# Head of a fused linear-attention and MLP kernel: values before the folded key weights

## The chip, the cores and the metric

The kernel runs on 1 core of a Trainium2 chip. The core has TensorE (PE), VectorE (DVE), ScalarE (ACT), GpSimd (POOL) and SyncE (SP), which run their own instruction queues and wait for one another by semaphores; DMAs are issued from SP's and ScalarE's queues here. The metric is the device time of one execution in microseconds, the median over runs. A measurement here tells differences of about 0.2% from none.

## The reference

Two branches read the same layer-normalised rows and are added to the input:

```python
def _A_ref(x, wqkv, w_phi, wo):
    B, S, D = x.shape
    H = 32; Dh = D // H
    qkv = (lambda x, *d: x.transpose(*d))((x @ wqkv).reshape(B, S, 3, H, Dh), 2, 0, 3, 1, 4)
    q, k, v = qkv[0], qkv[1], qkv[2]
    pq = jnp.einsum("bhsd,hdf->bhsf", q, w_phi)
    pk = jnp.einsum("bhsd,hdf->bhsf", k, w_phi)
    phi_q = jnp.concatenate([_softmax(pq, axis=-1), _softmax(-pq, axis=-1)], axis=-1)
    phi_k = jnp.concatenate([_softmax(pk, axis=-1), _softmax(-pk, axis=-1)], axis=-1)
    kv = jnp.einsum("bhsf,bhsd->bhfd", phi_k, v)
    z  = jnp.einsum("bhsf->bhf", phi_k)
    num = jnp.einsum("bhqf,bhfd->bhqd", phi_q, kv)
    den = jnp.einsum("bhqf,bhf->bhq", phi_q, z)[..., None] + 1e-6
    o = num / den
    return (lambda x, *d: x.transpose(*d))(o, 0, 2, 1, 3).reshape(B, S, D) @ wo

def _B_ref(x, w1, b1, w2):
    h = jnp.einsum("bsd,df->bsf", x, w1) + b1
    sp = jnp.log1p(jnp.exp(-jnp.abs(h))) + jnp.where(h > 0, h, jnp.zeros_like(h))
    act = h * jnp.tanh(sp)
    return jnp.einsum("bsf,fd->bsd", act, w2)

x = A_x
xn = _layernorm(x, axis=-1)
return x + _A_ref(xn, A_wqkv, A_w_phi, A_wo) + _B_ref(xn, B_w1, B_b1, B_w2)
```

S = 2048 rows, D = 512, 32 heads of 16, F = 1792, all bf16. The activation of the second branch is Mish.

## The kernel before

The 2048 rows are 16 tiles of 128, in 4 groups of 4. Everything stays on the core; only x and the weights come in and the result goes out. The order of the instructions on every engine is the order in which the code issues them (a manual schedule), so an instruction that waits holds back all that is issued behind it on its engine.

**The head (from line 420).** SP's queue issues x tiles 0 and 1, the key weights turned by a transposing DMA (`load_turned`), x tiles 4 to 7, the value weights `wv`, the first MLP weights `w1_sb`, and x tiles 8 to 15. ScalarE's queue issues `wsrc` (the per-head 16x16 maps), x tiles 2 and 3, and the bias `b1b`. GpSimd makes the identity and `block`, the mask of 16x16 blocks. VectorE copies three masks from `block`, and multiplies `block` with `wsrc` to the block-diagonal `Wbd`. TensorE runs 12 matmuls on the identity whose result nobody reads (`warm`). Then `fold` multiplies the turned key weights with `Wbd` to `wkp`, so that the key logits come out of one projection: 16 matmuls of 128 columns in four PSUM banks, each copied out.

`ln_stats` takes the layer norm's statistics on VectorE, and the power -1/2 on GpSimd; `ln_apply` applies them (on VectorE for groups 0 and 1, on GpSimd after). `ln_turn_pe` turns a tile by four TensorE transposes into a PSUM bank and a copy; from group 1 on, `normal` applies and turns by DMA. `project` is four matmuls of 512 columns: a tile's key logits (`logits`, with `wkp`) or its values (`value`, with `wv`, copied into `vext`). `hidden(n)` issues n units of the MLP's first layer: four matmuls of 512 columns and a Mish on ScalarE. There are 56 such units in all, and the calls share them out between the stages.

**The stages (loop from line 498).** For stage s, `exponentials(s)` takes the exponentials of a group's logits on ScalarE (two instructions for the halves k = 0, 1), `accumulate(s - 1)` adds a group's keys times values (32 matmuls of 129 columns), then come the values of group s (two tiles copied by VectorE, two by ScalarE), the logits of group s + 1, the statistics of group s + 2, `normalise` (a reduction, a reciprocal and a product on VectorE, for each half), the hidden units and `extremes(s + 1)`: the running max and min of the softmaxes, ten VectorE instructions in two planes. In stage 0 all four values of group 0 are done ahead of the loop, `extremes(0)` has `normal` of group 1 between its planes, and three tiles of the next logits go to a wide PSUM tile.

After the loop come the queries, the attention and the output projection, and the MLP's second layer; the change does not touch them.

**PSUM.** It has 8 banks. The pool `ps` has 5, handed out in turn to every projection, fold, transpose and hidden unit; the pool `ps2` has 3, for the wide tiles. An allocation waits until the bank's last content was copied out.

Of the kernel before, what the change touches and what calls it, by code (L numbers as in the profile page):

```python
# [8 lines left out]
BF16 = mybir.dt.bfloat16  # L9
FP32 = mybir.dt.float32  # L10

ACT = mybir.ActivationFunctionType
ALU = mybir.AluOpType
# [4 lines left out]
def kernel(  # L18
# [38 lines left out]
    vpool = ctx.enter_context(tc.tile_pool(name="vpool", bufs=1))  # L57
    opool = ctx.enter_context(tc.tile_pool(name="opool", bufs=2))
    ps = ctx.enter_context(tc.tile_pool(name="ps", bufs=5, space=bass.MemoryType.PSUM))
    ps2 = ctx.enter_context(tc.tile_pool(name="ps2", bufs=1, space=bass.MemoryType.PSUM))  # L60

    x_sb = persist.tile([P, NT, D], BF16, name="x_sb")
    xnT = persist.tile([P, NT, KT, P], BF16, name="xnT")
# [11 lines left out]
    wqp = wqk[:, :, 0:D]  # L75
    wo_sb = wqk[:, :, D : 2 * D]
    ident = consts.tile([P, P], BF16, name="ident")
    mhalf = consts.tile([P, TPG], FP32, name="mhalf")
    block = consts.tile([P, 8, 16], BF16, name="block")
    KVmask = consts.tile([P, 136], FP32, name="KVmask")  # L80
# [12 lines left out]
    def fold(wT, dst, dve):  # L93

        for kt in range(KT):
            pf = ps.tile([P, 512], FP32, name="pfold", tag="mm")
            for j in range(4):
                nc.tensor.matmul(
                    pf[:, j * P : (j + 1) * P],
                    lhsT=wT[:, j, kt * P : (kt + 1) * P],  # L100
                    rhs=Wbd[:, j, :],
                    start=True,
                    stop=True,
                )
            if kt in dve:
                nc.vector.tensor_copy(dst[:, kt, :], pf[:])
            else:
                nc.scalar.copy(dst[:, kt, :], pf[:])

    def ln_stats(t0, n):  # L110

        stats = lnp.tile([P, TPG, nc.vector.BN_STATS_DIM], FP32, name="stats")
        mv = lnp.tile([P, TPG, nc.vector.BN_AGGR_DIM], FP32, name="mv")
        rstd = lnp.tile([P, TPG], FP32, name="rstd")
        for i in range(n):
            nc.vector.bn_stats(stats[:, i, :], x_sb[:, t0 + i, :])  # L116
        for i in range(n):
            nc.vector.bn_aggr(mv[:, i, :], stats[:, i, :])
        nc.gpsimd.tensor_scalar(
            out=rstd[:, 0:n], in0=mv[:, 0:n, 1], scalar1=1e-5, scalar2=None, op0=ALU.add  # L120
        )
        nc.gpsimd.tensor_tensor(out=rstd[:, 0:n], in0=rstd[:, 0:n], in1=mhalf[:, 0:n], op=ALU.pow)
        return mv, rstd

    def ln_apply(t0, n, mv, rstd, xn, at):
        engine = nc.gpsimd if t0 > TPG else nc.vector
        for i in range(n):
            engine.tensor_scalar(  # L128
                out=xn[:, at + i, :],
                in0=x_sb[:, t0 + i, :],  # L130
                scalar1=mv[:, i, 0:1],
                scalar2=rstd[:, i : i + 1],
                op0=ALU.subtract,
                op1=ALU.mult,
            )

    def ln_turn_pe(t, xn, i, copy):
        ptr = ps.tile([P, 512], BF16, name="ptr", tag="mm")
        for kt in range(KT):
            nc.tensor.transpose(  # L140
                ptr[:, kt * P : (kt + 1) * P], xn[:, i, kt * P : (kt + 1) * P], ident[:]
            )
        copy(xnT[:, t, :, :], ptr[:].rearrange("p (k c) -> p k c", k=KT))
# [7 lines left out]
    def project(w, t, pp=None):  # L151

        if pp is None:
            pp = ps.tile([P, 512], FP32, name="pproj", tag="mm")[:]
        for kt in range(KT):
            nc.tensor.matmul(  # L156
                pp, lhsT=xnT[:, t, kt, :], rhs=w[:, kt, :],
                start=(kt == 0), stop=(kt == KT - 1),
            )
        return pp  # L160

    def value(t, copy):
        pv = project(wv, t)
        copy(
            vext[(t // TPG) % 2][:, t % TPG, :, 0:128], pv.rearrange("p (j c) -> p j c", j=4)
        )
# [3 lines left out]
    def hidden(n):  # L170

        for _ in range(n):
            g, f = next(units)
            ph = ps.tile([P, 512], FP32, name="ph", tag="mm")
            for kt in range(KT):
                nc.tensor.matmul(  # L176
                    ph[:],
                    lhsT=w1_sb[:, kt, f * P : (f + 1) * P],
                    rhs=xnT[:, g * TPG : (g + 1) * TPG, kt, :],
                    start=(kt == 0),  # L180
                    stop=(kt == KT - 1),
                )
            nc.scalar.activation(  # L183
                acts[:, f, g * 512 : (g + 1) * 512], ph[:], ACT.Mish, bias=b1f[:, f : f + 1]
            )
# [4 lines left out]
    def logits(s, i, copy):  # L190
        if i == 0:
            p_of[s] = smx.tile([P, TPG, 512], BF16, name="p_sb", bufs=1)
        pp = project(wkp if s < NG else wqp, (s % NG) * TPG + i)
        copy(p_of[s][:, i, :], pp)  # L194
# [222 lines left out]
        queue.dma_start(o_v[:, t, c], y)  # L417


    nc.sync.dma_start(x_sb[:, 0:2, :], x_v[:, 0:2, :])  # L420
    with nc.allow_non_contiguous_dma(reason="tiny w_phi load"):
        nc.scalar.dma_start(wsrc[:], wphi_v)
    wT = load_turned(D)
    nc.scalar.dma_start(x_sb[:, 2:4, :], x_v[:, 2:4, :])
    nc.scalar.dma_start(b1b[:], b1_v[:, :])
    nc.sync.dma_start(x_sb[:, 4:8, :], x_v[:, 4:8, :])
    nc.sync.dma_start(wv[:], wqkv_v[:, :, 2 * D : 3 * D])
    nc.sync.dma_start(w1_sb[:], w1_v[:, :, :])
    nc.sync.dma_start(x_sb[:, 8:16, :], x_v[:, 8:16, :])

# [10 lines left out]
    nc.gpsimd.memset(mhalf[:], -0.5)  # L441
    for i in range(2):
        nc.gpsimd.memset(vext[i][:, :, :, 128:136], 1.0)
    nc.vector.tensor_copy(KVmask[:, 0:P], block[:].rearrange("p h d -> p (h d)"))
    nc.vector.tensor_copy(KVmask[:, P : P + 8], block[:, :, 0])
    nc.vector.tensor_copy(
        kvm[:].rearrange("p l j c -> p (l j) c")[:, :, 136:144],
        block[:, None, :, 0].to_broadcast([P, 8, 8]),
    )
# [1 line left out]

    dve, act = nc.vector.tensor_copy, nc.scalar.copy

    warm = ps.tile([P, 4, P], FP32, name="warm", tag="mm")
    for _ in range(12):
        nc.tensor.matmul(
            warm[:], lhsT=ident[:], rhs=ident[:, None, :].to_broadcast([P, 4, P]),
            start=True, stop=True,
        )

    st0 = ln_stats(0, 2)
    nc.vector.tensor_tensor(
        out=Wbd[:].rearrange("p j (h e) -> p j h e", h=8),
        in0=block[:, None, :, :].to_broadcast([P, 4, 8, 16]),
        in1=wsrc[:, :, None, :].to_broadcast([P, 4, 8, 16]),
        op=ALU.mult,
    )
    st1 = ln_stats(2, 2)
    xn = lnp.tile([P, TPG, D], BF16, name="xn", tag="xn")
    ln_apply(0, 2, *st0, xn, 0)  # L470
    fold(wT, wkp, (3,))
    ln_turn_pe(0, xn, 0, dve)
    ln_turn_pe(1, xn, 1, act)
    pb = ps.tile([P, 512], BF16, name="pb", tag="mm")
    nc.tensor.transpose(pb[:, 0:FT], b1b[:], ident[0:FT, 0:FT])
    ln_apply(2, 2, *st1, xn, 2)
    logits(0, 0, act)
    for i in range(2, 4):
        ln_turn_pe(i, xn, i, dve)
    nc.vector.tensor_copy(b1f[:], pb[:, 0:FT])  # L480
    for i in range(1, TPG):
        logits(0, i, act)

    def normal(t0, st, xn):
        ln_apply(t0, TPG, *st, xn, 0)
        for i in (0, 2):
            ln_turn_dma(t0 + i, xn, i)

    st = ln_stats(TPG, TPG)
    xn = lnp.tile([P, TPG, D], BF16, name="xn", tag="xn")  # L490
    extremes(0, lambda: normal(TPG, st, xn))
    nc.sync.dma_start(w2_sb[:], w2_v[:, :, :])
    nc.sync.dma_start(wo_sb, wo_v[:, :, :])
    for i in range(TPG):
        value(i, act)
    hidden(5)

    for s in range(NG):
        exponentials(s, (0, 1) if s else (0,))
        if s > 0:  # L500
            accumulate(s - 1)
        if s < NG:
            for i in range(2 if s else 0):
                value(s * TPG + i, dve)
        if s == 0:
            p_of[1] = smx.tile([P, TPG, 512], BF16, name="p_sb", bufs=1)
            act(p_of[1][:, 0, :], project(wkp, TPG))
            exponentials(0, (1,))
            wide = ps2.tile([P, 3, 512], FP32, name="pwide", tag="kv")
            for i in range(3):  # L510
                project(wkp, TPG + 1 + i, wide[:, i, :])
        else:
            for i in range(TPG):
                logits(s + 1, i, act)
        if 0 < s < NG:
            for i in range(2, TPG):
                value(s * TPG + i, act)
        ln = s + 2 < NG
        if ln:
            t0 = (s + 2) * TPG  # L520
            st = ln_stats(t0, TPG)
            xn = lnp.tile([P, TPG, D], BF16, name="xn", tag="xn")
        elif s == 2:
            wT = load_turned(0)

        normalise(s, 0, (lambda: normal(t0, st, xn)) if ln else None)
        normalise(s, 1)
        if s == 2:
            fold(wT, wqp, ())
        if s == 0:  # L530
            hidden(6)
            act(p_of[1][:, 1:4, :], wide[:])
        hidden((11, 14, 8, 10)[s])
        extremes(s + 1)


# [76 lines left out]
```

## Time and profile before

| | |
|---|---|
| median of 3 runs | 183.92 us (183.82 to 184.01) |
| profiled execution, its own time | 183.6 us |
| span of its instructions | 181.9 us |
| TensorE busy | 175.4 us, of it 5.2 in the 12 `warm` matmuls |
| VectorE busy | 146.5 us |
| ScalarE busy | 126.5 us |
| GpSimd busy | 25.0 us |

The span runs from the first to the last instruction; the profiled execution's own time is longer by what lies around it. A row of the timeline gives the start, the duration of a run of like instructions, the engine, the line and operation, what it writes and reads, the count, and in brackets the idle time of the engine ahead of it and what ended that. A busy TensorE includes the overlap of a matmul with its predecessor's end, so matmuls are better counted by their steps from start to start. Where the text says "a chain", it is the page's own way back from the last instruction to what released it.

### The profile page before, as it was taken

Reading aid. Unit: us, or ns where it says so; the run is one execution under the profiler, and the core shown is the slowest. Engines: PE = TensorE matmul, PEld = TensorE weight load, DVE = VectorE, ACT = ScalarE, POOL = GpSimd, SP = SyncE. Lnnn points to the kernel's source line nnn. Section 1 sums busy time; section 2 is a strip of 40 time slices with the busy share of each in tenths; the row PEclk is TensorE's granted clock in tenths of the full one; section 3 lists DMA queues with packets and bytes.
Section 4 is the critical chain, followed back from the end, with each engine's and each line's share of the span. In section 5 each row is a group of like instructions: output and inputs, shape, how many; then the busy total and the mean of one; then the engine's idle time right before and its main releaser. Section 6 shows DMA issues by size and latency. Waiting matters only on the chain.

```text
span 181.9 us, 2744 instructions
## 1 busy us (share of the span) xinstructions
PE 175.4 (96%) x1024; PEld 90.2 (50%) x1039; DVE 146.5 (81%) x255; ACT 126.5 (70%) x194; POOL 25.0 (14%) x30
## 2 busy tenths in 40 slices
PE   6899999999999999999999999999999999999993
PEld 2454344465444645564465555455554545455561
DVE  2989979986999899988999786399916997647963
ACT  2367999999898899979986989472842558235300
POOL 4403079300793000000000000000000000000000
PEclk9999999999999999999999999999999999999999
DMA  6997796300023600000000840963079302990633
GB/s 145 291 401 267 160 356 175 60 0 5 0 50 65 119 0 0 0 0 4 0 0 0 153 81 10 189 147 63 0 171 203 88 5 41 200 192 31 76 101 115
DMA packets 44393, 18.02 MB, mean 99 GB/s; under 512 B 36828, under 2 KB 43868, under 8 KB 44380
## 3 DMA queue, kind: packets, MB, share of 16 engines
q1 hardware_dynamic: 43408, 17.50, 40.6%
q10 hardware_dynamic: 972, 0.35, 0.7%
q8 instruction: 8, 0.13, 0.3%
q14 instruction: 5, 0.04, 0.1%
HBM read 6.84 MB, written 2.10 MB: 49 GB/s over the span
## 4 chain that ended last, share of the span: by engine, by line
PE 78%; DVE 11%; ACT 4%; DMA 4%; issue 1%; DVEq 0%
PE po L399 22%; PE ph L176 22%; PE pproj L156 17%; PE po L408 7%; PE pkv L282 4%; PE pnd L326 4%; DVE stats L116 4%; ACT e L228 2%; DMA ob<-ob 2%; DMA x_sb<-in_A_x_dram 2%; DVE m L207 2%; DVE xn L128 1%; ACT L183 1%; DVE e L218 1%; DVE wkp L376 1%
## 5 line engine op out<-in xcount | busy, mean ns | idle before, releaser
L399 PE MATMUL po<-w_sb,acts 128*128 128x512 bf16 (+1 forms) x232 | 50.4, 366 | 0.3
L176 PE MATMUL ph<-xnT,w_sb 128*128 128x512 bf16 x224 | 49.5, 379 | 0.4 <-ACT acts L183 0.4
L183 ACT ACTIVATE acts<-ph,b1f 128x512 bf16<-128x512 f32 x56 | 35.2, 703 | 2.8 <-PE ph L176 2.6
L176 PEld LDWEIGHTS <-w_sb 128*128 128x128 bf16 x224 | 21.9, 98 | 26.7 <-issue 0.6
L228 ACT ACTIVATE e<-e 128x2048 bf16<-128x2048 bf16 x16 | 29.8, 1903 | 6.4 <-DVE e L218 6.3
L399 PEld LDWEIGHTS <-acts 128*128 128x128 bf16 x238 | 22.8, 98 | 22.0
L156 PEld LDWEIGHTS <-xnT 128*128 128x128 bf16 x192 | 18.3, 98 | 21.6 <-DMA xnT<-xn 0.8
L194 ACT CAST p_sb<-pproj 128x512 bf16<-128x512 f32 x25 | 13.7, 587 | 9.4 <-PE pproj L156 9.4
L416 DVE TENSOR_TENSOR x_sb<-po,x_sb 128x512 bf16<-128x512 f32 (+1 forms) x17 | 10.6, 655 | 11.4 <-PE po L408 11.4
L246 DVE TENSOR_REDUCE s<-e 128x128 f32<-128x2048 bf16 x8 | 18.2, 2278 | 1.9 <-ACT e L228 1.9
L128 POOL TENSOR_SCALAR xn<-x_sb,mv,rstd 128x512 bf16<-128x512 bf16 x8 | 16.7, 2100 | 0.2
L408 PE MATMUL po<-wqk,ob 128*128 128x512 bf16 (+1 forms) x66 | 14.7, 366 | 0.3 <-DMA ob<-ob 0.2
L156 PE MATMUL pproj<-wv,xnT 128*128 128x512 bf16 x61 | 14.8, 379 | 0.2
L156 PE MATMUL pproj<-wqk,xnT 128*128 128x512 bf16 x62 | 14.4, 379 | 0.1
L335 ACT CAST wkp<-pnd 128x768 bf16<-128x768 f32 x8 | 6.4, 798 | 11.3 <-PE pnd L326 7.4
L207 DVE TENSOR_TENSOR m<-m 128x512 bf16<-128x512 bf16 (+1 forms) x32 | 11.5, 359 | 1.1
L156 PE MATMUL pproj<-wkp,xnT 128*128 128x512 bf16 x50 | 11.8, 379 | 0.1
L207 DVE TENSOR_TENSOR m<-p_sb 128x1024 bf16<-128x1024 bf16 x16 | 11.0, 685 | 1.0 <-ACT p_sb L194 1.0
L326 PEld LDWEIGHTS <-qT 128*128 128x128 bf16 x128 | 9.1, 98 | 3.8
L116 DVE BATCH_NORM_STATS2 stats<-x_sb 128x6 f32<-128x512 bf16 x16 | 10.0, 679 | 1.2 <-DMA x_sb<-in_A_x_dram 1.2
L326 PE MATMUL pnd<-kvm,qT 128*128 128x144 bf16 x128 | 10.6, 226 | 0.0
L259 DVE TENSOR_TENSOR e<-e,r 128x2048 bf16<-128x2048 bf16 x8 | 10.3, 1281 | 0.3
(67 smaller groups left out, 175.2 us busy)
## 6 DMA issues: line engine op xcount, KB each, us to landing
w_sb<-in_B_w_dram SPq DMA_DIRECT2D x2, 1792.0 KB, 8.9
out_dram<-x_sb SPq DMA_DIRECT2D x15, 128.0 KB, 1.9
x_sb<-in_A_x_dram SPq DMA_DIRECT2D x1, 1024.0 KB, 11.7
x_sb<-in_A_x_dram SPq DMA_DIRECT2D x1, 512.0 KB, 4.0
wv<-in_A_wqkv_dram SPq DMA_DIRECT2D x1, 512.0 KB, 4.8
wqk<-in_A_wo_dram SPq DMA_DIRECT2D x1, 512.0 KB
x_sb<-in_A_x_dram SPq DMA_DIRECT2D x1, 256.0 KB, 3.2
x_sb<-in_A_x_dram ACTq DMA_DIRECT2D x1, 256.0 KB, 3.6
```

Source lines behind the costliest of these rows:

```text
L116: nc.vector.bn_stats(stats[:, i, :], x_sb[:, t0 + i, :])
L128: engine.tensor_scalar(out=xn[:, at + i, :], in0=x_sb[:, t0 + i, :], scalar1=mv[:, i, 0:1], scalar2=rstd[:, i : i + 1], op0=ALU.subtract, ...
L156: nc.tensor.matmul(pp, lhsT=xnT[:, t, kt, :], rhs=w[:, kt, :], start=(kt == 0), stop=(kt == KT - 1),)
L176: nc.tensor.matmul(ph[:], lhsT=w1_sb[:, kt, f * P : (f + 1) * P], rhs=xnT[:, g * TPG : (g + 1) * TPG, kt, :], start=(kt == 0), stop=(kt == ...
L183: nc.scalar.activation(acts[:, f, g * 512 : (g + 1) * 512], ph[:], ACT.Mish, bias=b1f[:, f : f + 1])
L194: copy(p_of[s][:, i, :], pp)
L207: nc.vector.tensor_tensor(out=m[:], in0=src[:, :, 0:half], in1=src[:, :, half : 2 * half], op=op)
L228: nc.scalar.activation(v, v, ACT.Exp)
L246: nc.vector.reduce_sum(t[:], v.rearrange("p t l (c e) -> p (t l c) e", e=16), axis=AX.X)
L326: nc.tensor.matmul(blocks(pnd, pl, j, 144), lhsT=qT_of[h][:, i, pl * 4 + j, :], rhs=kvm[:, pl, j, :], start=True, stop=True,)
L399: nc.tensor.matmul(po[:, c], lhsT=acts[:, f, t * P : (t + 1) * P], rhs=w2_sb[:, f, c], start=(f == 0), stop=False,)
L408: nc.tensor.matmul(po[:, c], lhsT=oT_of[h][:, t % 2 * 4 + j, :], rhs=wo_sb[:, j, c], start=False, stop=(j == 3),)
```

## The change

The loads are put in a new order: x tile 0 goes alone on SP and tile 1 on ScalarE's queue, `wv` follows on SP ahead of the turned key weights, `wsrc` comes third on ScalarE's queue, and `b1b` goes to SP behind x tiles 4 to 7. The three mask copies and `Wbd` move from VectorE to GpSimd. There are 10 `warm` matmuls instead of 12.

The layer norm of group 0 goes tile by tile (`spread` and `apply`): the root is a Sqrt on ScalarE and its reciprocal is VectorE's. One Sqrt is run early on a constant. Tiles 0 and 1 are turned and their values projected, tiles 2 and 3 are turned, then come the bias transpose, the fold (all four copies on ScalarE), values 2 and 3, and the four logits. The turned tiles, the bias and `warm` use a pool of three banks (`psh`), which is closed before `ps2` opens on the same banks.

`normal` of group 1 goes ahead of `extremes(0)`. Ahead of the loop there are 6 hidden units and no values. In stage 0, the projections of values 4 and 5 are issued behind the wide tile, and their copies (`keep`) on VectorE behind the first reduction; stage 1 then has only values 6 and 7. The hidden units of the stages are 9, 14, 9, 10 instead of 11, 14, 8, 10 (and 6 in stage 0 in both).

```diff
@@ -57,7 +57,8 @@
     vpool = ctx.enter_context(tc.tile_pool(name="vpool", bufs=1))
     opool = ctx.enter_context(tc.tile_pool(name="opool", bufs=2))
     ps = ctx.enter_context(tc.tile_pool(name="ps", bufs=5, space=bass.MemoryType.PSUM))
-    ps2 = ctx.enter_context(tc.tile_pool(name="ps2", bufs=1, space=bass.MemoryType.PSUM))
+    head = ExitStack()
+    psh = head.enter_context(tc.tile_pool(name="psh", bufs=3, space=bass.MemoryType.PSUM))
 
     x_sb = persist.tile([P, NT, D], BF16, name="x_sb")
     xnT = persist.tile([P, NT, KT, P], BF16, name="xnT")
@@ -75,6 +76,8 @@
     wqp = wqk[:, :, 0:D]
     wo_sb = wqk[:, :, D : 2 * D]
     ident = consts.tile([P, P], BF16, name="ident")
+    eps = consts.tile([P, 1], FP32, name="eps")
+    root = consts.tile([P, 1], FP32, name="root")
     mhalf = consts.tile([P, TPG], FP32, name="mhalf")
     block = consts.tile([P, 8, 16], BF16, name="block")
     KVmask = consts.tile([P, 136], FP32, name="KVmask")
@@ -135,7 +138,7 @@
             )
 
     def ln_turn_pe(t, xn, i, copy):
-        ptr = ps.tile([P, 512], BF16, name="ptr", tag="mm")
+        ptr = psh.tile([P, 512], BF16, name="ptr", tag="head")
         for kt in range(KT):
             nc.tensor.transpose(
                 ptr[:, kt * P : (kt + 1) * P], xn[:, i, kt * P : (kt + 1) * P], ident[:]
@@ -160,7 +163,9 @@
         return pp
 
     def value(t, copy):
-        pv = project(wv, t)
+        keep(t, project(wv, t), copy)
+
+    def keep(t, pv, copy):
         copy(
             vext[(t // TPG) % 2][:, t % TPG, :, 0:128], pv.rearrange("p (j c) -> p j c", j=4)
         )
@@ -417,14 +422,17 @@
         queue.dma_start(o_v[:, t, c], y)
 
 
-    nc.sync.dma_start(x_sb[:, 0:2, :], x_v[:, 0:2, :])
+    nc.gpsimd.memset(eps[:], 1e-5)
+    nc.sync.dma_start(x_sb[:, 0, :], x_v[:, 0, :])
+    nc.scalar.dma_start(x_sb[:, 1, :], x_v[:, 1, :])
+    nc.sync.dma_start(wv[:], wqkv_v[:, :, 2 * D : 3 * D])
+    nc.scalar.dma_start(x_sb[:, 2:4, :], x_v[:, 2:4, :])
     with nc.allow_non_contiguous_dma(reason="tiny w_phi load"):
         nc.scalar.dma_start(wsrc[:], wphi_v)
     wT = load_turned(D)
-    nc.scalar.dma_start(x_sb[:, 2:4, :], x_v[:, 2:4, :])
-    nc.scalar.dma_start(b1b[:], b1_v[:, :])
+    nc.scalar.activation(root[:], eps[:], ACT.Sqrt)
     nc.sync.dma_start(x_sb[:, 4:8, :], x_v[:, 4:8, :])
-    nc.sync.dma_start(wv[:], wqkv_v[:, :, 2 * D : 3 * D])
+    nc.sync.dma_start(b1b[:], b1_v[:, :])
     nc.sync.dma_start(w1_sb[:], w1_v[:, :, :])
     nc.sync.dma_start(x_sb[:, 8:16, :], x_v[:, 8:16, :])
 
@@ -441,9 +449,9 @@
     nc.gpsimd.memset(mhalf[:], -0.5)
     for i in range(2):
         nc.gpsimd.memset(vext[i][:, :, :, 128:136], 1.0)
-    nc.vector.tensor_copy(KVmask[:, 0:P], block[:].rearrange("p h d -> p (h d)"))
-    nc.vector.tensor_copy(KVmask[:, P : P + 8], block[:, :, 0])
-    nc.vector.tensor_copy(
+    nc.gpsimd.tensor_copy(KVmask[:, 0:P], block[:].rearrange("p h d -> p (h d)"))
+    nc.gpsimd.tensor_copy(KVmask[:, P : P + 8], block[:, :, 0])
+    nc.gpsimd.tensor_copy(
         kvm[:].rearrange("p l j c -> p (l j) c")[:, :, 136:144],
         block[:, None, :, 0].to_broadcast([P, 8, 8]),
     )
@@ -451,35 +459,61 @@
 
     dve, act = nc.vector.tensor_copy, nc.scalar.copy
 
-    warm = ps.tile([P, 4, P], FP32, name="warm", tag="mm")
-    for _ in range(12):
+    warm = psh.tile([P, 4, P], FP32, name="warm", tag="head")
+    for _ in range(10):
         nc.tensor.matmul(
             warm[:], lhsT=ident[:], rhs=ident[:, None, :].to_broadcast([P, 4, P]),
             start=True, stop=True,
         )
 
-    st0 = ln_stats(0, 2)
-    nc.vector.tensor_tensor(
+    nc.gpsimd.tensor_tensor(
         out=Wbd[:].rearrange("p j (h e) -> p j h e", h=8),
         in0=block[:, None, :, :].to_broadcast([P, 4, 8, 16]),
         in1=wsrc[:, :, None, :].to_broadcast([P, 4, 8, 16]),
         op=ALU.mult,
     )
-    st1 = ln_stats(2, 2)
+
     xn = lnp.tile([P, TPG, D], BF16, name="xn", tag="xn")
-    ln_apply(0, 2, *st0, xn, 0)
-    fold(wT, wkp, (3,))
-    ln_turn_pe(0, xn, 0, dve)
+    hstats = [lnp.tile([P, nc.vector.BN_STATS_DIM], FP32, name=f"hstats{i}", bufs=1) for i in range(4)]
+    hmv = [lnp.tile([P, nc.vector.BN_AGGR_DIM], FP32, name=f"hmv{i}", bufs=1) for i in range(4)]
+    hrstd = [lnp.tile([P, 1], FP32, name=f"hrstd{i}", bufs=1) for i in range(4)]
+
+    def spread(t):
+        nc.vector.bn_stats(hstats[t][:], x_sb[:, t, :])
+        nc.vector.bn_aggr(hmv[t][:], hstats[t][:])
+        nc.scalar.activation(hrstd[t][:], hmv[t][:, 1:2], ACT.Sqrt, bias=eps[:])
+
+    def apply(t):
+        nc.vector.reciprocal(hrstd[t][:], hrstd[t][:])
+        nc.vector.tensor_scalar(
+            out=xn[:, t, :], in0=x_sb[:, t, :], scalar1=hmv[t][:, 0:1], scalar2=hrstd[t][:],
+            op0=ALU.subtract, op1=ALU.mult,
+        )
+
+    spread(0)
+    spread(1)
+    apply(0)
+    ln_turn_pe(0, xn, 0, act)
+    apply(1)
     ln_turn_pe(1, xn, 1, act)
-    pb = ps.tile([P, 512], BF16, name="pb", tag="mm")
+    spread(2)
+    spread(3)
+    apply(2)
+    apply(3)
+    value(0, act)
+    value(1, act)
+    ln_turn_pe(2, xn, 2, dve)
+    ln_turn_pe(3, xn, 3, dve)
+    pb = psh.tile([P, 512], BF16, name="pb", tag="head")
     nc.tensor.transpose(pb[:, 0:FT], b1b[:], ident[0:FT, 0:FT])
-    ln_apply(2, 2, *st1, xn, 2)
-    logits(0, 0, act)
+    nc.vector.tensor_copy(b1f[:], pb[:, 0:FT])
+    fold(wT, wkp, ())
     for i in range(2, 4):
-        ln_turn_pe(i, xn, i, dve)
-    nc.vector.tensor_copy(b1f[:], pb[:, 0:FT])
-    for i in range(1, TPG):
+        value(i, act)
+    for i in range(4):
         logits(0, i, act)
+    head.close()
+    ps2 = ctx.enter_context(tc.tile_pool(name="ps2", bufs=1, space=bass.MemoryType.PSUM))
 
     def normal(t0, st, xn):
         ln_apply(t0, TPG, *st, xn, 0)
@@ -488,19 +522,18 @@
 
     st = ln_stats(TPG, TPG)
     xn = lnp.tile([P, TPG, D], BF16, name="xn", tag="xn")
-    extremes(0, lambda: normal(TPG, st, xn))
+    normal(TPG, st, xn)
+    extremes(0)
     nc.sync.dma_start(w2_sb[:], w2_v[:, :, :])
     nc.sync.dma_start(wo_sb, wo_v[:, :, :])
-    for i in range(TPG):
-        value(i, act)
-    hidden(5)
+    hidden(6)
 
     for s in range(NG):
         exponentials(s, (0, 1) if s else (0,))
         if s > 0:
             accumulate(s - 1)
         if s < NG:
-            for i in range(2 if s else 0):
+            for i in range(2 if s > 1 else 0):
                 value(s * TPG + i, dve)
         if s == 0:
             p_of[1] = smx.tile([P, TPG, 512], BF16, name="p_sb", bufs=1)
@@ -509,6 +542,7 @@
             wide = ps2.tile([P, 3, 512], FP32, name="pwide", tag="kv")
             for i in range(3):
                 project(wkp, TPG + 1 + i, wide[:, i, :])
+            ahead = [project(wv, TPG + i) for i in range(2)]
         else:
             for i in range(TPG):
                 logits(s + 1, i, act)
@@ -523,14 +557,21 @@
         elif s == 2:
             wT = load_turned(0)
 
-        normalise(s, 0, (lambda: normal(t0, st, xn)) if ln else None)
+        def amid():
+            if s == 0:
+                for i in range(2):
+                    keep(TPG + i, ahead[i], dve)
+            if ln:
+                normal(t0, st, xn)
+
+        normalise(s, 0, amid)
         normalise(s, 1)
         if s == 2:
             fold(wT, wqp, ())
         if s == 0:
             hidden(6)
             act(p_of[1][:, 1:4, :], wide[:])
-        hidden((11, 14, 8, 10)[s])
+        hidden((9, 14, 9, 10)[s])
         extremes(s + 1)
 
 
```

## The prediction

> **What bounds the kernel now.** I read the page's busy shares first, then its slices, then the chain that ended last, then the timeline of the first 50 us, because all the edits lie there.
>
> ```profile
> PE 175.4 (96%) x1024; PEld 90.2 (50%) x1039; DVE 146.5 (81%) x255; ACT 126.5 (70%) x194; POOL 25.0 (14%) x30
> ...
> PE   6899999999999999999999999999999999999993
> ...
> PE 78%; DVE 11%; ACT 4%; DMA 4%; issue 1%; DVEq 0%
> ```
>
> TensorE is full from the third slice to the end, and 78% of the chain is its own work. So time can only come from the holes of TensorE and from the useless work at its start: 12 warm-up matmuls. VectorE, at 81%, is the engine that may take over. The timeline of the head shows the holes:
>
> ```profile
> 4.00 1.29 DVE L116 BATCH_NORM_STATS2 stats<-x_sb 128x6 f32<-128x512 bf16 x2 [1.20 <-DMA x_sb<-in_A_x_dram]
> ...
> 6.67 0.90 PEld L98 LDWEIGHTS <-wT 128*128 128x128 bf16 x16 [0.86 <-DMA wT<-in_A_wqkv_dram]
> ...
> 8.52 0.38 PE L140 MATMUL ptr<-ident,xn 128*128 128x128 bf16 x4 [0.55 <-DVE wkp L106]
> ...
> 13.68 0.69 DVE L207 TENSOR_TENSOR m<-p_sb 128x1024 bf16<-128x1024 bf16 x1
> ```
>
> The first useful weight load waits for the turned key weights until 6.67; a transpose waits 0.55 for a bank that VectorE empties. At 13.68 VectorE starts `extremes(0)`: I call that moment S, and it decides this case. Later:
>
> ```profile
> 24.77 2.29 DVE L246 TENSOR_REDUCE s<-e 128x128 f32<-128x2048 bf16 x1 [1.11 <-ACT e L228]
> ...
> 29.07 10.52 PE L176 MATMUL ph<-xnT,w_sb 128*128 128x512 bf16 x48 [0.35 <-ACT acts L183]
> ...
> 39.43 1.98 PE L282 MATMUL pkv<-vext,e 128*128 128x129 bf16 x32
> ...
> 41.63 3.71 ACT L228 ACTIVATE e<-e 128x2048 bf16<-128x2048 bf16 x2
> 42.31 0.69 DVE L164 CAST vext<-pproj 128x512 bf16<-128x512 f32 x1 [1.96 <-PE pproj L156]
> ...
> 45.25 2.03 ACT L194 CAST p_sb<-pproj 128x512 bf16<-128x512 f32 x4
> ...
> 46.42 1.89 PE L156 MATMUL pproj<-wv,xnT 128*128 128x512 bf16 x8
> ```
>
> VectorE waits twice (1.11 and 1.96 us), TensorE 0.35. The logit copies of ScalarE (45.25) stand behind both exponentials (end 45.34); TensorE's values at 46.42 need banks that these copies free.
>
> **The head, step by step.** Unit prices: a 512-column matmul 0.216 (12.09 us for 56 in the chain of waits), so a unit of four 0.863; a transpose or fold matmul 0.056 (16 from 6.67 to about 7.56); a warm-up matmul 0.427 (weight loads at 2.24, 2.67, 3.09); about 0.17 more until the last result of a group is out, and 0.04 per hand-over.
>
> Warm-up: one memset ahead (0.03) puts its start at 1.44; ten steps end at 5.71 instead of 6.53.
>
> First tile: before, 256 KB landed at 4.00, sharing its time with another 256 KB and the small `wsrc` rows. Now 128 KB on each of two queues come first. Bounds for one: a 128 KB store lands 1.9 after issue, the 256 KB load 3.2; from 0.78 that is 2.7 to 4.0, and I take 3.3. VectorE: statistics 0.68, aggregate 0.16, the same for tile 1 (0.62 + 0.16), reciprocal, apply 0.40. The 128x1 reciprocal and ScalarE's 128x1 root are not in the trace: the reciprocal lies between 0.13 (128x64 copy) and 0.35 (128x32 reciprocal), the root between 0.22 (128x32 copy) and 0.70 (128x512 activation); I take 0.2 and 0.25, near the smallest rows. The root lies beside tile 1's statistics. Tile 0 is ready at 5.5, under the cover of the warm-up; a landing at 4.0 would bring 6.2 and cost 0.5.
>
> So TensorE turns tile 0 from 5.73, cold: out at 6.34; ScalarE's copy (0.59, row L143) ends at 6.97; value 0 starts at 7.02. Tile 1 goes beside it. Values 0 and 1: to 8.75. Tiles 2 and 3: eight transposes, 9.19. VectorE's two copies (0.41 each) end near 9.9. Bias transpose 9.25; fold 16 x 0.056, 10.14. Four fold copies on ScalarE from 9.68 cost 2.06 (row of the second fold), 11.74; values 2 and 3 hide them on TensorE until 11.87. Logits: 16 matmuls, 15.32; last copy to 16.11. **S = 16.15**, 2.5 later than before. The group of 1.38 applies and its statistics are done before S: VectorE has about 6 us between its last turned tile and S, and needs 2.5 + 0.4 + 1.3 (GpSimd's root) + 1.4.
>
> Queue orders behind this: `wv` is second on SP, 512 KB; its 4.8 from issue would give 6.1, before 7.02. The turned key weights are issued 0.5 later (issue 3.37, landing 5.3): about 7.2, or 7.7 with `wv` ahead of them; needed at 9.25. `b1b` moves from ScalarE's queue to SP behind all of these: 2.1 MB go ahead of it, which the rates of before, summed over the view of stretches, reach at 9.4 (1.94 MB by 9.0), less if the dip to 112 GB/s at 6.0 to 6.5 fills: 9.0. The fold stands behind it on TensorE, so this costs 0 to 0.5; I take 0. `w1_sb` keeps the bytes ahead of it (landed by 15.4 at the latest before) against a first use at 15.32. Three mask copies (0.74 on VectorE) and `Wbd` (0.39) go to GpSimd, whose nearest row, a 128x512 operation with one input, takes 2.09: `Wbd` from 5.2 to 7.3; twice that, 9.4, would cost 0.15. At the low end it is the VectorE price. None is on the path otherwise.
>
> A slower VectorE beside a busy GpSimd has one pair of rows in the trace: at 49.7 the r2 copy took 0.59 and the product behind it 1.67, against 0.29 and 1.23 elsewhere; at 28.1, with GpSimd busy too, they took 0.29 and 1.23. For the applies beside `Wbd` I take 0 of it, and 0.3, the copy's excess, as the far end.
>
> [...]
>
> **From S to the end.** TensorE at 15.32 has done what it had done at 16.31 before: 0.99 ahead. To `accumulate(0)` it has 27 units, 23.3 us, to 38.6. The hole of 0.35 goes, since the banks of the two early values come back at 28.6 (below) before they are needed. That is 0.81 earlier than 39.43, with one unit (two values in, one hidden out) more done: a lead of 1.7.
>
> VectorE from S, with times of the same pieces before: `extremes(0)` 5.96 without its middle (2.98 a plane); statistics 2.74; reduction 2.31; two value copies 1.28, new here; reciprocal to product 2.46; the second half 2.31 + 2.46; `extremes(1)` 6.04. Sum 25.56: **41.7**, against 40.36 before. The wait of 1.11 is gone: the first exponential ends S + 8.45, the reduction wants it at S + 8.70. Then both exponentials 3.71 and the first logit copy 0.57: TensorE's sixth bank in this stage comes free at S + 29.85 = 46.0. The sixth allocation is value 7. TensorE is there after `accumulate(0)` 1.81, 16 logit matmuls and value 6: 44.7. **It waits 1.3 us**; before, the two values at the stage's start kept this place for 47.2, when the bank was long free. That is where most of the lead goes. After value 7, the 14 hidden units start at 46.86 against 48.15: 1.29 less, minus the unit that stage 2 now has more (0.86), leaves 0.43. With no further holes that is the result. VectorE, with its two copies gone from stage 1 and the wait of 1.96 too, is 1.6 us ahead in stages 2 and 3, so the end follows TensorE.
>
> So delta = S - 16.58: break-even is S at 16.58. The profiled execution took 183.6 with a span of 181.9; 183.6 - 0.4 = 183.2, and the median of the runs lies 0.3 above the profiled one: **183.5**.
>
> **Rivals.**
> 1. *The clock of TensorE* (slower). Warm-up matmuls step at 0.427, later ones at 0.216: the faster rate came only inside the twelfth, which took 0.51 instead of 0.62, so at about 6.5. Now ten are left, then transposes, then a hole of 0.5. If the rate rises only after values 0 and 1, their eight matmuls cost 1.7 more: S = 17.85, 1.3 slower, 185.2. It decides from 0.4 of delay. For it: nothing in the trace shows the rate rising in under 5 us of matmuls. Against: at 6.5 TensorE would have been busy without a hole. [...]
> 2. *The wait at value 7 doesn't come* (faster): if VectorE's chain is shorter than summed, TensorE keeps 1.7: 182.2. For it: TensorE sets most of the chain. Against: the sum's pieces are all measured.
> 3. *Late constants* (the change is not what it says, a head free of waits): `b1b`, `Wbd` or contention hold the fold by 0.8: S = 16.95, 0.4 slower, 184.3. For it: `b1b` stands behind 2.1 MB. Against: the estimate of 9.0 to 9.4.
>
> **How the numbers follow.** Forecast 0.45, its own range 183.0 to 184.1 (S from 15.7 to 16.75); rival 1 0.22; rival 2 0.20; rival 3 0.13. A measurement of this kernel can tell about 0.2%, 0.37 us, from no change: below 183.55 is faster, above 184.29 slower. Faster: 0.25 of the forecast + 0.20 = 0.45. Same: 0.18 + 0.04 = 0.22. Slower: 0.02 + 0.22 + 0.09 = 0.33. Range 182.2 (rival 2) to 185.4 (rival 1 with 0.2 of contention).
>
> **What would show it.** Right: value 0 near 7.0, the first m of line L207 near 16.2, `accumulate(0)` near 38.6, a hole of about 1.3 on TensorE before the last value matmuls near 46, and no waits of 1.11 and 1.96 on VectorE. Wrong: values 0 and 1 at 0.43 per matmul (rival 1); no hole near 46 (rival 2); the bias transpose waiting for `b1b` (rival 3); roots on ScalarE bringing extra table loads, 1.28 each by the page's rows.

## The result, and the profile after

The change makes the kernel slower: 185.01 us in the median of 6 runs (184.38 to 185.25) against 183.82 before (six runs too), a ratio of 1.006 (95% interval 1.0048 to 1.0072). The profiled execution took 184.75 us with a span of 183.0; the one before had 183.6 and 181.9.

The page's busy shares, the slices of TensorE and the chain that ended last, as they are now:

```profile
PE 176.1 (96%) x1037; PEld 90.0 (49%) x1037; DVE 145.9 (80%) x253; ACT 129.1 (71%) x201; POOL 24.4 (13%) x31
...
PE   6979999999899999999999999999999999999993
...
PE 70%; DVE 11%; DMA 7%; SPq 4%; ACT 3%; issue 2%; DVEq 0%
```

TensorE is as full as before, but the third slice (9.2 to 13.7) has fallen to 7, and SP's queue and a DMA have come into the chain with 11% where DMA alone had 4%. The timeline of the head names them:

```profile
1.72 4.55 SPq L93 DMA_TRANSPOSE wT<-in_A_wqkv_dram  x1
...
6.61 0.69 DVE L482 BATCH_NORM_STATS2 hstats<-x_sb 128x6 f32<-128x512 bf16 x1 [0.46 <-DMA x_sb<-in_A_x_dram]
6.93 1.15 POOL L469 TENSOR_TENSOR Wbd<-block,wsrc 128x512 bf16<-128x512 bf16 x1 [3.62 <-DMA wsrc<-in_A_w_phi_dram]
6.95 0.53 SPq L435 DMA_DIRECT2D b1b<-in_B_b_dram  x1
...
7.00 2.07 PE L159 MATMUL pproj<-wv,xnT 128*128 128x512 bf16 x8 [0.18 <-ACT xnT L146]
...
8.90 0.89 PE L143 MATMUL ptr<-ident,xn 128*128 128x128 bf16 x8
...
10.69 0.18 PE L508 MATMUL pb<-ident,b1b 14*128 14x14 bf16 x1 [0.90 <-DMA b1b<-in_B_b_dram]
...
10.80 1.07 PE L101 MATMUL pfold<-Wbd,wT 128*128 128x128 bf16 x16
```

Value 0 starts at 7.00. Then SP is seen to need 4.55 us for the issue of the turned key weights, so that the 3.5 KB of `b1b` are issued at 6.95. TensorE waits 0.90 for them with the bias transpose, and the fold stands behind it, at 10.80. Nothing else held the fold: `Wbd` ends at 8.08 (6.93 + 1.15), and the turned key weights landed 6.6 after their issue at 1.72, at 8.3. From S on:

```profile
17.40 5.35 PE L181 MATMUL ph<-xnT,w_sb 128*128 128x512 bf16 x24 [0.36 <-DMA w_sb<-in_B_w_dram]
...
17.70 0.69 DVE L212 TENSOR_TENSOR m<-p_sb 128x1024 bf16<-128x1024 bf16 x1 [1.09 <-ACT p_sb L199]
...
26.73 2.29 DVE L251 TENSOR_REDUCE s<-e 128x128 f32<-128x2048 bf16 x1 [0.33 <-ACT e L233]
...
47.03 2.02 ACT L199 CAST p_sb<-pproj 128x512 bf16<-128x512 f32 x4
...
47.65 1.02 PE L159 MATMUL pproj<-wv,xnT 128*128 128x512 bf16 x4 [0.63 <-ACT p_sb L199]
```

S is 17.70 instead of 13.68. VectorE's wait at the first reduction is 0.33 instead of 1.11. Value 7 is issued alone at 47.65, after a wait of 0.63 for the logit copies at 47.03: the new hole in stage 1.

### The profile page after: what moved, and what is told of

It reads as the page before. It is cut to its first block, busy times and chain, and to the rows that moved or that the text cites. A ratio compares the mean times of both kernels' runs of the same rounds, so it can differ in the third digit from the quotient of the medians.

```text
span 183.0 us, 2760 instructions
## 1 busy us (share of the span) xinstructions
PE 176.1 (96%) x1037; PEld 90.0 (49%) x1037; DVE 145.9 (80%) x253; ACT 129.1 (71%) x201; POOL 24.4 (13%) x31
## 4 chain that ended last, share of the span: by engine, by line
PE 70%; DVE 11%; DMA 7%; SPq 4%; ACT 3%; issue 2%; DVEq 0%
PE po L404 22%; PE ph L181 19%; PE pproj L159 14%; PE po L413 7%; DMA w_sb<-in_B_w_dram 5%; PE pnd L331 4%; PE pkv L287 3%; SPq L93 2%; DVE s L251 2%; ACT e L233 2%; DMA ob<-ob 2%; DVE m L212 1%; DVE e L223 1%; DVE e L264 1%; DVE r L259 1%
## 5 line engine op out<-in xcount | busy, mean ns | idle before, releaser
L188 ACT ACTIVATE acts<-ph,b1f 128x512 bf16<-128x512 f32 x56 | 35.7, 695 | 4.7 <-PE ph L181 4.4
L199 ACT CAST p_sb<-pproj 128x512 bf16<-128x512 f32 x25 | 13.7, 586 | 8.6 <-PE pproj L159 8.6
L159 PE MATMUL pproj<-wv,xnT 128*128 128x512 bf16 x64 | 15.5, 382 | 0.8 <-ACT p_sb L199 0.6
L340 ACT CAST wv<-pnd 128x768 bf16<-128x768 f32 x8 | 6.3, 790 | 5.9 <-PE pnd L331 3.7
```

The costliest lines, as they stand in the source:

```text
L159: nc.tensor.matmul(pp, lhsT=xnT[:, t, kt, :], rhs=w[:, kt, :], start=(kt == 0), stop=(kt == KT - 1),)
L188: nc.scalar.activation(acts[:, f, g * 512 : (g + 1) * 512], ph[:], ACT.Mish, bias=b1f[:, f : f + 1])
L340: nc.scalar.copy(to[:, :, 0:3, :], a)
```

## The experiments

Each edit is against the changed kernel unless it says otherwise; the ratios are against the kernel before, run beside it. Medians are compared with medians, and profiled executions with profiled executions.

**1. b1b back on ScalarE's queue.**

```diff
+    nc.scalar.dma_start(b1b[:], b1_v[:, :])
     nc.scalar.activation(root[:], eps[:], ACT.Sqrt)
...
-    nc.sync.dma_start(b1b[:], b1_v[:, :])
```

> The changed kernel with b1b back on ScalarE's queue, behind wsrc. Theory (the bias transpose waits for b1b and holds the fold behind it): the wait of 0.9 goes, the fold starts at 9.8 behind the turned tiles, S (start of extremes(0)) falls from 17.7 to 16.7. The first MLP weights are issued 0.6 earlier but still land at about 16.5, so the hidden units wait 0.6 there and the first exponential holds the reduction some 0.3. Time 184.1 (183.8 to 184.4). Rival (the fold is held by the turned key weights or by Wbd, or the time is lost elsewhere): fold still at 10.5 or later, 185.0 as with the change.

Measured 183.32 us (183.04 to 183.9, 11 runs), ratio 0.998 (0.997 to 0.999). The timeline of this run, its head and its stage 1:

```profile
8.99 0.92 PE L143 MATMUL ptr<-ident,xn 128*128 128x128 bf16 x8 [0.23 <-DVE xn L488]
...
9.84 0.18 PE L508 MATMUL pb<-ident,b1b 14*128 14x14 bf16 x1
...
16.85 0.69 DVE L212 TENSOR_TENSOR m<-p_sb 128x1024 bf16<-128x1024 bf16 x1
...
46.35 1.02 PE L159 MATMUL pproj<-wv,xnT 128*128 128x512 bf16 x4 [0.71 <-ACT p_sb L199]
```

The bias transpose no longer waits, the fold starts at 9.95 (expected 9.8), S is 16.85 (16.7). The one line is worth 1.7 us and turns the change from slower to slightly faster. Two things were not as expected. The hidden units start at 16.03, and only their first weight load waits 0.27 for the first MLP weights; and the total is 0.8 below the expected time. The profiled execution, 183.43, is 0.17 below that of before and 1.32 below that of the change: the 0.90 at the bias transpose and the 0.36 at the first hidden unit make up 1.26 of it. That the second wait belongs to the place of `b1b` is not shown, as in edit 2, with `b1b` still on SP, the first hidden unit does not wait either (16.18). What is left late in the head is x tiles 2 and 3, for which tile 2's turn waits 0.23.

**2. The bias transpose behind the logits**, loads untouched.

```diff
-    pb = psh.tile([P, 512], BF16, name="pb", tag="head")
-    nc.tensor.transpose(pb[:, 0:FT], b1b[:], ident[0:FT, 0:FT])
-    nc.vector.tensor_copy(b1f[:], pb[:, 0:FT])
     fold(wT, wkp, ())
...
         logits(0, i, act)
+    pb = psh.tile([P, 512], BF16, name="pb", tag="head")
+    nc.tensor.transpose(pb[:, 0:FT], b1b[:], ident[0:FT, 0:FT])
+    nc.vector.tensor_copy(b1f[:], pb[:, 0:FT])
```

> The changed kernel with the bias transpose and its copy issued behind the four logits instead of ahead of the fold; loads untouched. Theory: the fold starts at 9.8 and S is 16.7 here too, so the queue position of the transpose is what made the wait matter. The first MLP weights still land at 17.2, so the hidden units now wait 1.3 instead of 0.4, and the first exponential with them: the wait moves, and the time is 184.7 (184.3 to 185.0). Rival (S alone decides): 184.0.

Measured 188.43 us, ratio 1.0247 (1.0229 to 1.0266): far off. The timeline shows that the edit made a wait of its own:

```profile
9.90 1.06 PE L101 MATMUL pfold<-Wbd,wT 128*128 128x128 bf16 x16
...
16.29 0.17 DVE L514 CAST b1f<-pb 128x14 f32<-128x14 bf16 x1 [5.76 <-PE pb L513]
16.38 2.46 DVE L119 BATCH_NORM_STATS2 stats<-x_sb 128x6 f32<-128x512 bf16 x4
...
24.60 1.04 PE L159 MATMUL pproj<-wkp,xnT 128*128 128x512 bf16 x3 [3.07 <-DMA xnT<-xn]
```

The fold does start at 9.90, as expected. But the 0.17 us copy of the bias now waits 5.76 on VectorE, and group 1's statistics stand behind it, from 16.38 instead of 11: S is 21.90, and TensorE waits 3.07 for the turned tiles. The total says nothing of the theory; the fold's start supports it. The expected wait of 1.3 at the hidden units did not come.

**3. One hidden unit from stage 2 to stage 0.**

```diff
-        hidden((9, 14, 9, 10)[s])
+        hidden((10, 14, 8, 10)[s])
```

> The changed kernel with one hidden unit moved from stage 2 to stage 0 (10, 14, 8, 10). Theory (TensorE waits in stage 1 for the bank of value 7 because the two values are gone from the stage's start): the unit fills that wait of 0.6 to 0.9, time 184.3 (184.0 to 184.5). Rival (the later VectorE chain sets the end in any case): 185.0, no change.

Measured 184.14 us (183.79 to 185.11, 12 runs), ratio 1.0021 (1.0009 to 1.0033): 0.87 below the change, as expected. The profiled execution was the slowest of the twelve, 185.11; there SP's issue of the turned key weights took 5.52 and the bias transpose came at 11.78. The values 6 and 7 are together again:

```profile
1.71 5.52 SPq L93 DMA_TRANSPOSE wT<-in_A_wqkv_dram  x1
...
47.70 2.19 PE L159 MATMUL pproj<-wv,xnT 128*128 128x512 bf16 x8
```

Eight matmuls in 2.19 instead of 1.89: of the hole 0.3 is left in this execution.

**4. The turned key weights ahead of wv.**

```diff
-    nc.sync.dma_start(wv[:], wqkv_v[:, :, 2 * D : 3 * D])
...
     wT = load_turned(D)
+    nc.sync.dma_start(wv[:], wqkv_v[:, :, 2 * D : 3 * D])
```

> The changed kernel with the turned key weights issued ahead of wv on SP, so only that order is undone. Theory (the 512 KB of wv in front lengthened the issue of the transposing load from 3.4 to 4.6 and with it delayed everything behind it on SP): the issue falls back to about 3.4, x tiles 4 to 7 are issued near 5.6, the first MLP weights near 6.8 and land by 16; but wv lands at 8.0 to 9.0, so value 0 starts 1 to 2 later, and the fold is no earlier than 10.3. S 17.2 to 18.0, the wait for the MLP weights gone: 184.8 (184.4 to 185.3). Rival (the issue is longer for a reason of its own): issue still 4.5, time 185.5 or more.

Measured 186.83 us, ratio 1.0165 (1.0147 to 1.0182): right on the issue, wrong on the price.

```profile
1.25 3.05 SPq L93 DMA_TRANSPOSE wT<-in_A_wqkv_dram  x1
...
8.97 3.42 PE L159 MATMUL pproj<-wv,xnT 128*128 128x512 bf16 x8 [2.19 <-DMA wv<-in_A_wqkv_dram]
```

The same run by stretches (start and end, length, the share of its full clock that TensorE was granted, DMA share, GB/s):

```profile
8.00:9.00 1.00, 1.00 1.08 382
9.00:10.00 1.00, 0.58 1.09 364
10.00:11.00 1.00, 0.50 1.01 405
```

The issue takes 3.05, against 4.55 in the changed kernel. So `wv` in front is what lengthens it. But after the hole of 2.19 the eight value matmuls take 3.42; from the second on they are 0.43 apart. This is the price of the prediction's first rival, but not its course: the eight transposes ahead of the hole ran at the fast rate (0.056 apart, from 5.86), and the granted clock then fell, from 1.00 to 0.50. The values cost 1.5 more than the 1.90 that they take in edit 1, which is most of the 2 us by which the expectation was short.

**5. b1b on ScalarE's queue and the hidden unit moved** (edits 1 and 3).

> b1b on ScalarE's queue and one hidden unit moved from stage 2 to stage 0 (10, 14, 8, 10). Theory (two separate costs, the wait for b1b in the head and the wait of 0.7 for the bank of value 7 in stage 1, which add): 182.6 (182.3 to 182.9). Rival (both are the same slack, and once the head is shorter VectorE's chain sets the end): 183.3, as with b1b alone.

Measured 182.71 us (182.41 to 182.74), ratio 0.9938 (0.9926 to 0.995). The two costs add: 0.6 below edit 1. In this run's profile values 6 and 7 are together, eight matmuls in 2.19 as in edit 3, so 0.3 of the hole is left here too. This version beats both kernels.

**6. As 5, and the fold ahead of the turns of tiles 2 and 3.**

```diff
     value(1, act)
+    fold(wT, wkp, ())
     ln_turn_pe(2, xn, 2, dve)
...
-    fold(wT, wkp, ())
```

> As e5_b1b_hidden10, and the fold issued on TensorE right behind value 1, ahead of the turns of tiles 2 and 3. Theory (in the head with b1b early, TensorE waits for x tiles 2 and 3, which land 2 us later than before; the turned key weights are there by 8.7): the fold fills that wait, S falls from 16.9 to 16.1, but the hidden units then wait about 0.6 for the first MLP weights near 15.9: 182.2 (181.9 to 182.6). Rival (the turned key weights land after 9, so the fold itself waits): 182.6 or more.

Measured 182.55 us (182.34 to 183.08), ratio 0.994 (0.9927 to 0.9953): not to be told from 5. The fold starts at 8.69, a microsecond earlier than in 5, but value 2 only at 10.49, against 10.56, behind a wait of 0.19 for ScalarE's copies of the fold; S is 16.50, against 16.77 in 5 and 16.1 expected. The wait that the fold was to fill is missing from 5's own profile: there x tiles 2 and 3 landed 3.8 after their issue (5.5 in edit 1), and tile 2's turn at 9.01 waits for nothing. The key weights were not waited for either, so the runs decide for neither theory.

**7. The two early values undone**, with b1b on ScalarE's queue.

```diff
-    hidden(6)
+    hidden(5)
...
-            for i in range(2 if s > 1 else 0):
+            for i in range(2 if s else 0):
...
-            ahead = [project(wv, TPG + i) for i in range(2)]
...
-            if s == 0:
-                for i in range(2):
-                    keep(TPG + i, ahead[i], dve)
...
-        hidden((9, 14, 9, 10)[s])
+        hidden((11, 14, 8, 10)[s])
```

> b1b on ScalarE's queue, and the two early values undone: values 4 and 5 back at the start of stage 1, their copies out of stage 0, hidden units as before (5, then 11, 14, 8, 10). Theory (the two early values take VectorE 1.3 us in stage 0 and make TensorE wait in stage 1): no wait of TensorE near 46, time 182.9 (182.6 to 183.2), 0.4 below b1b alone. Rival (the early values are worth something by removing VectorE's wait of 2 us in stage 1): 183.6 or more.

Measured 183.39 us (183.07 to 184.35, 11 runs), ratio 0.9989 (0.9977 to 1.0): the same as edit 1, between the two theories. The wait near 46 is gone, but two holes are back in stage 0 at the places where the kernel before has 0.37 (on a weight load, at 20.67) and 0.35:

```profile
20.98 1.04 PE L159 MATMUL pproj<-wkp,xnT 128*128 128x512 bf16 x4 [0.45 <-DMA xnT<-xn]
...
29.19 10.52 PE L181 MATMUL ph<-xnT,w_sb 128*128 128x512 bf16 x48 [0.26 <-ACT acts L188]
```

Their 0.45 and 0.26 are together the 0.71 of the wait for value 7 in edit 1. So, by these two profiles, the early values close two holes and open one of the same size; only with the tenth unit (edit 5) is there a gain.

**8. The masks and Wbd back on VectorE**, with b1b on ScalarE's queue; the four calls go from `nc.gpsimd` to `nc.vector`, and `Wbd` stands behind `apply(3)`.

```diff
-    nc.gpsimd.tensor_copy(KVmask[:, 0:P], block[:].rearrange("p h d -> p (h d)"))
+    nc.vector.tensor_copy(KVmask[:, 0:P], block[:].rearrange("p h d -> p (h d)"))
...
     apply(3)
+    nc.vector.tensor_tensor(
+        out=Wbd[:].rearrange("p j (h e) -> p j h e", h=8),
...
```

> b1b on ScalarE's queue, and the three mask copies and Wbd back on VectorE (Wbd behind the applies of tiles 2 and 3). Theory (GpSimd's part costs and gains nothing: the masks lie in idle time, and Wbd is ready before the fold either way): 183.3 (183.1 to 183.6), the same as b1b alone. Rival (VectorE loses beside a busy GpSimd): 183.0 or less; rival (Wbd on VectorE holds the copies of the turned tiles): 183.7 or more.

Measured 183.52 us (183.17 to 184.04), ratio 0.9987 (0.9976 to 0.9998), an interval that overlaps that of edit 1; the medians lie 0.2 apart. GpSimd's part costs and gains nothing that these runs can tell.

**9. The kernel before, with b1b alone moved to SP.**

```diff
-    nc.scalar.dma_start(b1b[:], b1_v[:, :])
     nc.sync.dma_start(x_sb[:, 4:8, :], x_v[:, 4:8, :])
+    nc.sync.dma_start(b1b[:], b1_v[:, :])
```

> The kernel before with only b1b moved, from ScalarE's queue to SP behind x tiles 4 to 7. Theory (on SP the small load lands with the 512 KB ahead of it, so the bias transpose holds TensorE): b1b lands at 9.2 to 9.5 instead of before 8.8, the bias transpose waits 0.4 to 0.6 and the logits behind it: 184.3 (184.1 to 184.5). Rival (b1b's queue matters only behind the lengthened issue of the turned key weights): 183.8, no change.

Measured 184.02 us (183.87 to 184.29, 11 runs), ratio 1.0011 (1.0003 to 1.002).

```profile
9.47 0.18 PE L475 MATMUL pb<-ident,b1b 14*128 14x14 bf16 x1 [0.62 <-DMA b1b<-in_B_b_dram]
...
23.54 1.90 PE L156 MATMUL pwide<-wkp,xnT 128*128 128x512 bf16 x8 [0.31 <-DMA xnT<-xn]
25.28 14.95 PE L176 MATMUL ph<-xnT,w_sb 128*128 128x512 bf16 x68
```

The wait is there, 0.62, at the expected place. In the medians it costs 0.2, between the two theories; why it costs no more is not shown. The profile does not explain it: the 17 hidden units run without the hole of 0.35 that the kernel before has at 29.07, but a new wait of 0.31 stands at 23.54, `accumulate(0)` starts at 40.06, 0.63 after that of before, and the profiled execution, the slowest of the eleven at 184.29, is 0.69 above that of before.

**10. As 6, with hidden units 11, 14, 7, 10.**

> As e6_fold_early with the hidden units 11, 14, 7, 10. Theory (0.3 of the wait for the bank of value 7 is left with 10): one unit more fills it: 182.3 (182.1 to 182.6). Rival (stage 2, with 7 units, becomes too short for VectorE): 182.6 or more.

Measured 183.22 us (183.05 to 183.53), ratio 0.997 (0.9958 to 0.9982): 0.7 worse than 6, the rival.

```profile
84.16 1.02 PE L159 MATMUL pproj<-wv,xnT 128*128 128x512 bf16 x4 [0.51 <-ACT p_sb L199]
```

In stage 3 the last value now waits 0.51 for ScalarE's logit copies, a wait that 6 does not have. The copies stand behind the exponentials, so I read it as the rival says: with 7 units TensorE is through stage 2 too soon for VectorE.

**11. As 5, with 6 warm-up matmuls.**

```diff
-    for _ in range(10):
+    for _ in range(6):
```

> As e5_b1b_hidden10 with 6 warm-up matmuls instead of 10. Theory (TensorE's faster rate comes only after some microseconds of matmuls, and 10 are near the edge): TensorE is idle from 4.0 to 5.7, the values of tiles 0 and 1 step at 0.43 instead of 0.22, S is up to 1.7 later than in e5: 183.8 (183.2 to 184.5). Rival (turns and short waits keep the rate's rise where it was): 182.7, as e5.

Measured 183.61 us (182.58 to 184.61, 12 runs), ratio 0.9991 (0.9972 to 1.0009): 0.9 above 5 in the median.

```profile
6.94 3.08 PE L159 MATMUL pproj<-wv,xnT 128*128 128x512 bf16 x8 [0.16 <-ACT xnT L146]
```

Eight value matmuls take 3.08 instead of 1.90, with no wait inside: the first five ran at the slow rate. The twelve runs spread over 2.0 us, the five of edit 5 over 0.3.

## Why the prediction was wrong, by its own steps

**The step that failed** is "`b1b` moves from ScalarE's queue to SP behind all of these ... The fold stands behind it on TensorE, so this costs 0 to 0.5; I take 0." It cost 0.90 of waiting on TensorE. Under it lies "the turned key weights are issued 0.5 later (issue 3.37 ...)": the duration was carried over from a queue in which nothing large stood in front. With 512 KB of `wv` there it was 4.55, so x tiles 4 to 7 were issued at 6.32 instead of 5.2 (1.8 + 3.37), `b1b` at 6.95 and the MLP weights at 7.53. The byte sum failed with it: the dip at 6.0 to 6.5 did fill, but the rates stayed low beside the turning, which landed 6.6 us after its issue instead of 5.3. The same view of stretches, before and after:

```profile
7.00:8.00 1.00, 1.00 1.07 371
```

```profile
6.00:6.50 0.50, 1.00 1.19 220
6.50:7.00 0.50, 1.00 1.27 276
7.00:8.00 1.00, 1.00 1.25 245
8.00:9.00 1.00, 1.00 0.85 244
```

Before, the stretches from 7 to 8 and 8 to 9 had 371 and 355 GB/s; after, 245 and 244. Summed up, those of after reach 2.1 MB at about 9.7. The x tiles 4 to 7, issued just ahead of `b1b`, landed 4.1 after their issue, at 10.4, and TensorE got the bias at 10.7. So a byte sum is not a landing time: here about 1.0 lay between the two, and what it consists of is in no run shown.

**A second, smaller miss:** x tiles 2 and 3 were not costed at all. Their 256 KB landed 5.4 after issue instead of 3.6, so VectorE waited 0.46 for them, and the turns ended at 9.79 instead of 9.19. That `wv` beside them delays them is supported by edit 4, where `wv` is issued at 4.35 and they landed 3.2 after issue; with `wv` in front it was 3.8 (edit 5) to 6.2 (edit 3), by the execution. The 1.55 by which S was late is all there when the fold starts, at 10.80 instead of 9.25: 0.60 from the turns, 0.90 from `b1b`, the rest at the hand-over. Edit 1 shows the first part alone: S 16.85 against the predicted 16.15.

**Right, with numbers:** the warm-up's end, the first tile and value 0 (7.00, predicted 7.02). The 27 units from the first hidden unit to `accumulate(0)` took 23.3, as summed (17.40 to 40.72). The wait of 1.11 on VectorE went, as costed; I put down the 0.33 that took its place to the late MLP weights, on which the prediction had left no wait. The wait for the bank of value 7: predicted 1.3, measured 0.63, because TensorE lost time before it; one unit moved ahead of it is worth 0.87 in edit 3 and 0.61 between edits 1 and 5. The roots on ScalarE brought no table loads (13 of 1.28 us in both profiles) and took 0.29, predicted 0.25. `Wbd` on GpSimd took 1.15, about half of the row of 2.09 that stood in for it.

**Right in part by luck:** the rule "delta = S - 16.58". With S at 17.70 it gives 1.12, and the profiled executions differ by 1.15. But edit 1, with S at 16.85, should by it be 0.27 slower than before and is 0.17 faster. The sum has value 7's bank free at S + 29.85. Value 7 starts at S + 29.95 in the changed kernel, and at S + 29.5 in edits 1, 2, 4 and 8, in whose profiles VectorE does not wait at the first reduction. So the sum is some 0.35 too long, and the 0.33, which it did not have, made it come out.

**The rivals.** Rival 3, late constants with `b1b` first among them, is what happened, at 1.55 of S instead of 0.8: right in mechanism, half the size. It got 0.13 because the byte sum was taken as a landing time. Rival 1, the clock, came in by its edge: the first value matmul took 0.56 instead of 0.38, about 0.2 us in all, in the changed kernel's profile; in those of edits 1 to 3, 5 to 8 and 10, with the same ten warm-up matmuls, it took 0.38 to 0.39. Edit 11 shows most of its price when the warm-up is cut (1.2 for the eight values), and in edit 4, behind a hole of 2.19, the values cost 1.5 more although the rate had risen before. Rival 2 fell: the wait at value 7 came.

## What to carry to other kernels

A small load that an in-order engine needs early is to be judged by the queue it stands in, not by its size: here it came just after what was ahead of it (10.7 behind x tiles that landed at 10.4), and one forgotten consumer (here a transpose of 14 rows) holds all that is behind it. When loads are reordered, the issue times of the others change too (3.37 became 4.55 for the turned key weights), so every duration taken from the old queue wants a bound above. And when work is moved between stages, the units that fill the stages are to be moved with it: here one unit of 0.86 us was worth 0.6 to 0.9, and the next one cost 0.7 (edit 10).

## What the runs showed of the hardware

The issue of a transposing load on SP took 3.05 to 3.37 us in three profiles with only an x load of 128 or 256 KB ahead of it (the kernel before, edits 4 and 9) and 4.48 to 5.52 in ten with the 512 KB of `wv` ahead, and in those it varied from run to run. `b1b` was in time on ScalarE's queue (no wait in the kernel before and in edit 1) and late on SP's behind x tiles 4 to 7 (TensorE waited 0.90 in the changed kernel, 0.62 in edit 9). The length of the issue is in no run explained further.

TensorE's fast rate came at different times in the profiled executions, though the ten warm-up matmuls were the same and began at 1.44 to 1.45. The warm-up of the changed kernel and of edit 1:

```profile
1.45 4.45 PE L464 MATMUL warm<-ident 128*128 128x512 bf16 x10 [1.45 <-POOL ident masks.py:199]
```

```profile
1.45 3.69 PE L464 MATMUL warm<-ident 128*128 128x512 bf16 x10 [1.45 <-POOL ident masks.py:199]
```

In the changed kernel the rate rose only with the first value matmul, after 7.0; in edit 1 it rose inside the warm-up, whose steps go from 0.43 to 0.22 at about 4.3. The other profiles with ten warm-up matmuls lie between, and their first values ran at the fast rate (eight in 1.89 or 1.90), but for edit 4, where the granted clock had fallen to 0.50. With 6 warm-up matmuls the first five of the eight values ran at the slow rate, 0.43 apart. What sets the time of the rise is in no run shown, nor whether it makes the spread of 2.0 us in edit 11, of whose twelve runs one was profiled.
